# Output weights of the first group loaded in the last batch and split in place, a gate in four steps, and no conversion in a batch's first step

## The chip, the cores and the metric

The kernel runs on one core of a Trainium2 chip. The metric is device time in microseconds (us) of one execution, from the host's launch to the end, as the median of several runs. The engines are named as the profile names them: PE multiplies matrices, PEld loads its stationary operand, DVE, ACT and POOL are the vector, scalar and GpSimd engines, and SP issues most of the transfers. Each engine takes its instructions in the order in which they stand in its own queue.

## The reference

An attention, a mixture of experts over its output, and a last MLP. Cut to what matters here:

```python
def _attn_ref(q, k, v, p):                  # 4 batches, 8 heads, 576 tokens, head_dim 64
    p_packed = sm_attn(p, k, v)
    return sm_attn(q, p_packed, p_packed)

def _moe_ref(x, domain_probs, w1, w2):      # x (2304, 512), 4 experts, F = 1024
    p = domain_probs / (domain_probs.sum(-1, keepdims=True) + 1e-09)
    for e in range(E):
        h = np.maximum(x @ w1[e], 0.0)
        out += p[:, e:e + 1] * (h @ w2[e])

def _moe2_ref(x, w_in, w_out, s, b):        # w_in (512, 2048), w_out (2048, 512), both float64
    h = x @ w_in
    r = np.maximum(h, 0.0)
    g = s * (r * r) + b
    return (g @ w_out).astype(np.float32)
```

## The kernel before

Every float32 operand of a matmul is split into a high part (rounded to the multiplier's format by ACT) and a low part (the rest, by DVE or POOL), and each product is three matmuls: low by high, high by high, high by low.

**The expert loop** has 256 steps: 4 experts, 4 batches of 576 tokens, and 16 steps a batch (two halves of 288 tokens, 8 blocks of hidden columns each). A step runs the work woven into it (`run(i)`), then `m1` (L578), the first product of the step that comes two later, then `m2` (L605), the second product of its own step. `m1` ends with ACT's `hh` (L596) and DVE's `hl` (L597), which read the PSUM tile `h`. There are two such tiles, so the `m1` of two steps later cannot begin before that `hl` is done. A batch's last `m2` is followed by four evictions on DVE (`y`, L629). For an even batch the folded first weights (`fold_pair`, L419: PE, then ACT L434 and DVE L435 twice) are made during the batch before, one piece in each of eight steps, and the last piece falls in the batch's own first step.

**The conversion** (`last_weights`, L463) turns the float64 words of `w_in` and `w_out` into float32 by operations on integers. It has 32 tiles, each with a load and three parts: exponent (L485, L488), significand (L493 to L496), product (L502, POOL L505, and a store to `wi_dram` or `wo_dram`). The list `calm` holds the steps that may take a part. A part runs ahead of its step's `m1`, so DVE and ACT have it in their queues ahead of that step's `hh` and `hl`.

**The MLP** works in 4 groups of 512 hidden columns, each in 3 batches of 768 tokens. A batch has 14 products (`m3`, L715): 7 operands of a Strassen scheme, named 11, 12, s2, s3, s1, s4 and 22, for two column blocks `j`. I number the products through, p0 to p13 for the first batch, p14 to p27 for the second. p0 to p9 are run in the last steps of the expert loop (`EARLY`). DVE adds the products into `yy`. With s4 (p10, p11) and 22 (p12, p13) a piece of `yy` is complete and goes through the gate: ACT's Relu and Square (L703, L704), DVE's scale (L692), ACT's high part (L693), DVE's low part (L696). `go_on` (L708) takes every piece that is under way one step further after each product:

```python
    def gate(g, tp, j, c):
        nc.scalar.activation(y, y, AF.Relu)
        nc.scalar.activation(y, y, AF.Square)
        gg[g, tp, j, c] = t
        later.append([(gate_hi, y, t), (gate_lo, y, t)])
```

The output product `m4` (L757) of a batch is 72 matmuls: 6 tiles of 128 tokens, 12 matmuls each. They are dealt out from two products after the batch's end, some 5 behind each product: those of the first batch stand behind p16 to p29, those of the second behind p30 and on. The PSUM tiles `o` are two; in the first group ACT copies each to `o_sb` (L776), in the later groups DVE adds it there (L780). After the last product of all, PE runs what is left, 82 matmuls or so.

`m4` needs the group's output weights `wo`, four tiles. `load_wo` (L551) reads one from `wo_dram` on SP's queue into the raw tile `wor`, of which there are two, and `wo_parts` (L555) splits it: ACT L560 and POOL L561. For the first group both stand behind the end of the expert loop. SP's queue also holds the stores of the split operands `xs` to `xs_dram` (L684), each of which waits for DVE's low part (L683) of that operand.

Of the kernel before, what the change touches and what calls it, by code (L numbers as in the profile page):

```python
# [8 lines left out]
F32 = mybir.dt.float32  # L9
F32R = mybir.dt.float32r  # L10
U32 = mybir.dt.uint32
AF = mybir.ActivationFunctionType
ALU = mybir.AluOpType
# [6 lines left out]
def attention_experts_mlp_kernel(  # L20
# [25 lines left out]
    nc = tc.nc  # L46
    B, H, S, D = q.shape
    NP = p.shape[2]
    NT, DM = out.shape
    E, _, F = w1.shape  # L50
    DFF = w_out.shape[0]
    P = 128
    G = 2
    HT = S // 2
    NF = F // P
# [5 lines left out]
    T3 = 384  # L61
    NT3 = NT // T3
    NS = T3 // P
    FG = 4
# [4 lines left out]
    keep = ctx.enter_context(tc.tile_pool(name="keep", bufs=1))  # L69
# [10 lines left out]
    def f32(ap):  # L80
        return ap.bitcast(F32)
# [269 lines left out]
    w1_t, w1p, w2_t, wi_t, wo_t = {}, {}, {}, {}, {}  # L351
# [103 lines left out]
    NQ = FG // 2  # L455
# [5 lines left out]
    wo_dram = [dram.tile([P, DM], F32, name=f"wo_dram{fb}") for fb in range(DFF // P)]  # L461
# [46 lines left out]

        return load, exponent, significand, product

    tw, wop, wor = {}, {}, {}

    def load_wi(q):
        g = q // NQ
# [33 lines left out]
            nc.scalar.activation(t[:, j, 0], src, AF.Copy)  # L548
            nc.vector.tensor_tensor(out=t[:, j, 1], in0=src, in1=f32(t[:, j, 0]), op=ALU.subtract)

    def load_wo(fb):  # L551
        wor[fb] = gb.tile([P, DM], F32, tag="wor", bufs=2, name=f"wor{fb}")
        nc.sync.dma_start(out=wor[fb], in_=wo_dram[fb])

    def wo_parts(fb):  # L555
        pool, tag = (keep, "w1p") if fb // FG % 2 == 0 else (gb, "wo")
        t = pool.tile([P, 2, DM], F32R, tag=tag, bufs=FG, name=f"wo{fb}")
        hi, lo = wo_t[fb] = t[:, 0], t[:, 1]
        raw = wor.pop(fb)
        nc.scalar.activation(hi, raw, AF.Copy)  # L560
        nc.gpsimd.tensor_tensor(out=lo, in0=raw, in1=f32(hi), op=ALU.subtract)  # L561


    pb_t = {}
# [78 lines left out]
    xs, gg, o_acc, o_sb, sx, yy = {}, {}, {}, {}, {}, {}  # L643
# [44 lines left out]

    cur, later = {}, []

    def gate_hi(y, t):
        nc.vector.tensor_scalar(y, y, s_sb, b_sb, ALU.mult, ALU.add)  # L692
        nc.scalar.activation(t[:, 0], y, AF.Copy)  # L693

    def gate_lo(y, t):
        nc.vector.tensor_tensor(out=t[:, 1], in0=y, in1=f32(t[:, 0]), op=ALU.subtract)  # L696

    def gate(g, tp, j, c):


        y = yy[j][:, 2 * c : 2 * c + 2, :]
        t = gb.tile([P, 2, 2, T3], F32R, tag="gg", bufs=6, name=f"gg{g}{tp}{j}{c}")
        nc.scalar.activation(y, y, AF.Relu)  # L703
        nc.scalar.activation(y, y, AF.Square)  # L704
        gg[g, tp, j, c] = t
        later.append([(gate_hi, y, t), (gate_lo, y, t)])

    def go_on():  # L708
        for x in list(later):
# [5 lines left out]
    def m3(g, tp, k, j):  # L715
        op, name = OPS[k], f"{g}{tp}{k}{j}"
        n = cur["n"] = cur.get("n", -1) + 1
        if (g, tp) == (0, 0) and 2 * k + j < EARLY:
            ps = ps_m.tile([P, 512], F32, tag="m", name=f"h{name}")
        elif n % 3 == 0:  # L720
            ps = ps_h.tile([P, 512], F32, tag="h", name=f"h{name}")
        else:
            ps = ps_o.tile([P, 512], F32, tag="c", bufs=4, name=f"h{name}")
        ps = ps[:, :T3]
        w, x = wop[g, k][:, j], xs[g, tp, k]
        n = 0
        for m in range(HK):
            col = slice(m * P, (m + 1) * P)
            for a, z in ((1, 0), (0, 0), (0, 1)):
                nc.tensor.matmul(  # L730
                    ps, lhsT=w[:, a, col], rhs=x[:, z, m, :],
                    start=(n == 0), stop=(n == 3 * HK - 1),
                )
                n += 1
        if op == "11":
            yy[j] = wb.tile([P, 4, T3], F32, tag="yy", bufs=NQ, name=f"yy{name}")
            cur[j] = wb.tile([P, 2, T3], F32, tag="uv", bufs=NQ, name=f"uv{name}")
        y = yy[j]
        u, v = cur[j][:, 0], cur[j][:, 1]
        if op == "11":  # L740
            nc.scalar.activation(u, ps, AF.Copy)
        for dst, src in {
            "12": ((y[:, 0], u),),
            "s2": ((u, u),),
            "s3": ((v, u),),
            "s1": ((y[:, 1], u), (y[:, 3], v)),
            "s4": ((y[:, 1], y[:, 1]),),
            "22": ((y[:, 2], v),),
        }.get(op, ()):
            nc.vector.tensor_tensor(out=dst, in0=ps, in1=src, op=ALU.add)  # L750
        go_on()
        if op in ("s4", "22"):
            gate(g, tp, j, int(op == "22"))

    EARLY = 10
# [30 lines left out]
    with tc.manual_schedule():  # L786
# [3 lines left out]
        for gi in range(G):  # L790
# [4 lines left out]
            out=dp.rearrange("a j e -> a (j e)"),  # L795
            in_=probs.rearrange("(a j) e -> a (j e)", a=P),
# [88 lines left out]
        for gi in range(G):  # L885
# [3 lines left out]
        ua = [  # L889
            (e, bi, hf, f) for e in range(E) for bi in range(B) for hf in range(2) for f in range(NF)  # L890
        ]
# [15 lines left out]
        SB = 2 * NF  # L907

        def at(step, fn, *args):
            weave.setdefault(step, []).append((fn, args))  # L910
# [68 lines left out]
        for j in range(2):  # L979
# [1 line left out]

        calm = [
            e * B * SB + i for e in range(1, E) for i in range(3 * SB)
            if not SB + NF <= i < 2 * SB and (e < E - 1 or i < 2 * SB)
        ]
        tiles = [
            (w, g * FG + f) for g in range(NG) for w in ("wi", "wo") for f in range(FG)
# [15 lines left out]
        def pos(v):  # L1003

            return len(ua) + v - EARLY
# [1 line left out]
        for k in range(4, NK):  # L1007
            at(len(ua) - 8 + 2 * (k - 4), wop_parts, 0, k)
        for f in range(FG):
            at(pos(EARLY) + f, load_wo, f)  # L1010
            at(pos(EARLY) + 2 + f, wo_parts, f)
        for tp in range(NTP):
            u0 = tp * UP
            for d, what in enumerate(("s1", "s2", "s3")):
# [111 lines left out]
```

## Time and profile before

| what | value |
|---|---|
| runs, median (lowest to highest) | 1163.51 us (1163.32 to 1163.72) |
| the profiled execution's own time | 1165.72 us |
| its span, first to last instruction | 1163.9 us |
| busy: PE / DVE / ACT / POOL | 1114.5 / 697.9 / 453.9 / 278.5 us |
| mean granted PE clock, as a share of full speed | 0.988 |

PE is busy for 96% of the span, so what can still go are the stretches in which it waits, and those in which it runs at the lower clock. The profiled execution is 2.2 us longer than the median of the runs, and 1.8 us of its time lie outside its span.

### The profile page before, as it was taken

Reading aid. Unit: us, or ns where it says so; the run is one execution under the profiler, and the core shown is the slowest. Engines: PE = TensorE matmul, PEld = TensorE weight load, DVE = VectorE, ACT = ScalarE, POOL = GpSimd, SP = SyncE. Lnnn points to the kernel's source line nnn. Section 1 sums busy time; section 2 is a strip of 40 time slices with the busy share of each in tenths; the row PEclk is TensorE's granted clock in tenths of the full one; section 3 lists DMA queues with packets and bytes.
Section 4 is the critical chain, followed back from the end, with each engine's and each line's share of the span. In section 5 each row is a group of like instructions: output and inputs, shape, how many; then the busy total and the mean of one; then the engine's idle time right before and its main releaser. Section 6 shows DMA issues by size and latency. Waiting matters only on the chain.

```text
span 1163.9 us, 18380 instructions
## 1 busy us (share of the span) xinstructions
PE 1114.5 (96%) x7243; PEld 1043.4 (90%) x7243; DVE 697.9 (60%) x1276; ACT 453.9 (39%) x860; POOL 278.5 (24%) x337
## 2 busy tenths in 40 slices
PE   6899999999999999999999999979899999999997
PEld 4788998999999999999999999968789989998996
DVE  7767655466666576566576344557645666566554
ACT  3322222363343363343453333344454444334232
POOL 1421302133413342413244124425110200011000
PEclk9999999999999999999999999989899999999999
DMA  8622220223303324304233002235565655655532
GB/s 252 170 80 81 58 83 1 66 91 120 120 1 125 123 67 134 93 28 154 76 95 99 1 14 88 120 134 199 196 224 186 203 185 201 218 189 186 201 121 82
DMA packets 60150, 141.51 MB, mean 122 GB/s; under 512 B 8864, under 2 KB 29600, under 8 KB 60064
## 3 DMA queue, kind: packets, MB, share of 16 engines
q1 hardware_dynamic: 59792, 140.28, 36.9%
q8 instruction: 57, 0.93, 0.3%
q14 instruction: 29, 0.24, 0.1%
q10 hardware_dynamic: 272, 0.07, 0.0%
HBM read 110.66 MB, written 29.66 MB: 121 GB/s over the span
## 4 chain that ended last, share of the span: by engine, by line
PE 83%; DVE 7%; ACT 5%; issue 2%; DMA 1%; POOL 1%; SPq 0%; DVEq 0%; ACTq 0%; POOLq 0%
PE acc L614 33%; PE h L586 17%; PE o L764 14%; PE h L730 12%; PE pp L425 3%; ACT yy L703 1%; ACT yy L704 1%; PE s L288 1%; ACT gg L693 1%; PE pw L368 1%; DVE yy L692 1%; PE s L180 1%; DVE yy L750 1%; PE pv L234 1%; DMA w2r<-in_moe_w_dram 1%
## 5 line engine op out<-in xcount | busy, mean ns | idle before, releaser
L614 PE MATMUL acc<-hh,w2l 128*128 128x288 f32 x1024 | 304.3, 297 | 1.2 <-DVE sc L299 0.6
L614 PE MATMUL acc<-hl,w2h 128*128 128x288 f32 x1024 | 303.7, 297 | 0.0
L614 PE MATMUL acc<-hh,w2h 128*128 128x288 f32 x1024 | 303.5, 296 | 0.0
L586 PE MATMUL h<-a,w1p 128*128 128x288 f32 x1536 | 253.3, 301 | 10.4 <-DVE hl L597 7.7
L764 PE MATMUL o<-wo,gg 128*128 128x512 f32 x864 | 228.6, 397 | 21.2 <-POOL wo L561 9.8
L586 PEld LDWEIGHTS h<-a,w1p 128*128 128x128 f32 x1536 | 219.3, 190 | 19.8 <-DVE hl L597 9.1
L597 DVE SCALAR_TENSOR_TENSOR hl<-h,hh 128x288 fp32r<-128x288 f32 x256 | 116.5, 456 | 174.9 <-ACT hh L596 173.1
L764 PEld LDWEIGHTS o<-wo,gg 128*128 128x128 f32 x864 | 161.1, 189 | 50.3 <-POOL wo L561 11.9
L730 PE MATMUL h<-xs,wop 128*128 128x384 f32 x1008 | 206.0, 341 | 0.0
L614 PEld LDWEIGHTS acc<-hh,w2l 128*128 128x128 f32 x1024 | 193.3, 189 | 2.5 <-POOL w2l L450 1.2
L730 PEld LDWEIGHTS h<-xs,wop 128*128 128x128 f32 x1008 | 182.8, 190 | 13.1 <-DVE y L629 0.3
L614 PEld LDWEIGHTS acc<-hl,w2h 128*128 128x128 f32 x1024 | 193.8, 189 | 0.0
L614 PEld LDWEIGHTS acc<-hh,w2h 128*128 128x128 f32 x1024 | 193.6, 189 | 0.0
L596 ACT ACTIVATE hh<-h 128x288 fp32r<-128x288 f32 x256 | 103.9, 408 | 223.1 <-PE h L586 221.1
L640 POOL TENSOR_TENSOR x<-x,y 128x288 f32<-128x288 f32 (+2 forms) x144 | 87.7, 644 | 183.9 <-DVE y L629 183.9
L435 DVE TENSOR_TENSOR w1p<-pp,w1p 64x512 fp32r<-64x512 f32 x96 | 66.1, 688 | 53.7 <-ACT w1p L434 53.0
L703 ACT ACTIVATE yy<-yy 128x768 f32<-128x768 f32 x48 | 40.0, 834 | 115.3 <-DVE yy L750 115.3
L434 ACT ACTIVATE w1p<-pp 64x512 fp32r<-64x512 f32 x96 | 56.7, 591 | 70.2 <-DVE w1p L435 43.4
L750 DVE TENSOR_TENSOR yy<-h,uv 128x384 f32<-128x384 f32 x96 | 50.5, 551 | 26.7 <-PE h L730 26.3
L450 POOL TENSOR_TENSOR w2l<-w2r,w2h 128x512 fp32r<-128x512 f32 x32 | 41.6, 1300 | 86.8 <-ACT w2h L449 63.0
L696 DVE TENSOR_TENSOR gg<-yy,gg 128x768 fp32r<-128x768 f32 x48 | 51.2, 1066 | 18.2 <-ACT gg L693 18.2
L693 ACT ACTIVATE gg<-yy 128x768 fp32r<-128x768 f32 x48 | 40.6, 845 | 47.0 <-DVE yy L692 43.0
(361 smaller groups left out, 1100.9 us busy)
## 6 DMA issues: line engine op xcount, KB each, us to landing
xs<-xs_dram SPq DMA_DIRECT2D x63, 768.0 KB, 4.3
xs_dram<-xs SPq DMA_DIRECT2D x21, 768.0 KB, 3.3
w2r<-in_moe_w_dram SPq DMA_DIRECT2D x32, 256.0 KB, 2.8
w1r<-in_moe_w_dram SPq DMA_DIRECT2D x12, 512.0 KB, 4.0
pb<-pn_dram SPq DMA_DIRECT2D x16, 288.0 KB, 4.5
out_dram<-o_sb SPq DMA_DIRECT2D x17, 256.0 KB, 2.1
v<-in_v_dram SPq DMA_DIRECT2D x8, 512.0 KB, 5.7
wi<-wi_dram SPq DMA_DIRECT2D x8, 512.0 KB, 5.2
```

The costliest lines, as they stand in the source:

```text
L434: nc.scalar.activation(hi[r], t[r], AF.Copy)
L435: nc.vector.tensor_tensor(out=lo[r], in0=t[r], in1=f32(hi[r]), op=ALU.subtract)
L586: nc.tensor.matmul(t[:, :HT], lhsT=w[:, gi, col], rhs=a2[bi][:, x, gi, tok], start=(n == 0), stop=(n == 3 * G - 1),)
L596: nc.scalar.activation(xh, t[:, :HT], AF.Relu)
L597: nc.vector.scalar_tensor_tensor(out=xl, in0=t[:, :HT], scalar=0.0, in1=f32(xh), op0=ALU.max, op1=ALU.subtract)
L614: nc.tensor.matmul(acc[m][:, :HT], lhsT=w[:, col], rhs=x, start=(f == 0 and n == 0), stop=(f == NF - 1 and n == 2),)
L640: nc.gpsimd.tensor_tensor(out=dst, in0=dst, in1=y[:, a - t0 : z - t0], op=ALU.add)
L693: nc.scalar.activation(t[:, 0], y, AF.Copy)
L703: nc.scalar.activation(y, y, AF.Relu)
L730: nc.tensor.matmul(ps, lhsT=w[:, a, col], rhs=x[:, z, m, :], start=(n == 0), stop=(n == 3 * HK - 1),)
L750: nc.vector.tensor_tensor(out=dst, in0=ps, in1=src, op=ALU.add)
L764: nc.tensor.matmul(o_acc[i], lhsT=lhsT, rhs=w, start=(f == 0 and n == 0), stop=(f == FG - 1 and n == 2),)
```

## The change

Three things are changed.

The list `calm` leaves out each batch's first step (`i % SB`). All 32 tiles still fit, and the conversion now ends at step 215 instead of 207.

The first group's `wo` tiles are loaded in steps 250 and 253 of the expert loop, by transfers that ACT's queue issues, and split from step 254 on. In all groups the raw weights land in the low half of their own tile; ACT writes the high half from it, and POOL subtracts in place. The raw tiles `wor` are gone.

The gate has four steps instead of Relu and Square at once and two more: Relu with Square one product later, scale after two, high part after three, low part after four. Since a piece is then still under way when the next batch begins, `yy` and `uv` are allocated once and not anew for each batch.

```diff
-    def load_wo(fb):
-        wor[fb] = gb.tile([P, DM], F32, tag="wor", bufs=2, name=f"wor{fb}")
-        nc.sync.dma_start(out=wor[fb], in_=wo_dram[fb])
-
-    def wo_parts(fb):
+    def load_wo(fb, eng=nc.sync):
         pool, tag = (keep, "w1p") if fb // FG % 2 == 0 else (gb, "wo")
         t = pool.tile([P, 2, DM], F32R, tag=tag, bufs=FG, name=f"wo{fb}")
-        hi, lo = wo_t[fb] = t[:, 0], t[:, 1]
-        raw = wor.pop(fb)
-        nc.scalar.activation(hi, raw, AF.Copy)
-        nc.gpsimd.tensor_tensor(out=lo, in0=raw, in1=f32(hi), op=ALU.subtract)
+        eng.dma_start(out=f32(t[:, 1]), in_=wo_dram[fb])
+        wo_t[fb] = t[:, 0], t[:, 1]
+
+    def wo_parts(fb):
+        hi, lo = wo_t[fb]
+        nc.scalar.activation(hi, f32(lo), AF.Copy)
+        nc.gpsimd.tensor_tensor(out=lo, in0=f32(lo), in1=f32(hi), op=ALU.subtract)
...
-    def gate_hi(y, t):
-        nc.vector.tensor_scalar(y, y, s_sb, b_sb, ALU.mult, ALU.add)
-        nc.scalar.activation(t[:, 0], y, AF.Copy)
...
+    def gate_act(y, key):
         nc.scalar.activation(y, y, AF.Relu)
         nc.scalar.activation(y, y, AF.Square)
-        gg[g, tp, j, c] = t
-        later.append([(gate_hi, y, t), (gate_lo, y, t)])
+
+    def gate_scale(y, key):
+        nc.vector.tensor_scalar(y, y, s_sb, b_sb, ALU.mult, ALU.add)
+
+    def gate_hi(y, key):
+        name = "gg" + "".join(map(str, key))
+        t = gg[key] = gb.tile([P, 2, 2, T3], F32R, tag="gg", bufs=6, name=name)
+        nc.scalar.activation(t[:, 0], y, AF.Copy)
+
+    def gate_lo(y, key):
+        t = gg[key]
+        nc.vector.tensor_tensor(out=t[:, 1], in0=y, in1=f32(t[:, 0]), op=ALU.subtract)
+
+    def gate(g, tp, j, c):
...
+        later.append([(fn, y, (g, tp, j, c)) for fn in (gate_act, gate_scale, gate_hi, gate_lo)])
...
-        if op == "11":
-            yy[j] = wb.tile([P, 4, T3], F32, tag="yy", bufs=NQ, name=f"yy{name}")
-            cur[j] = wb.tile([P, 2, T3], F32, tag="uv", bufs=NQ, name=f"uv{name}")
+        if j not in yy:
+            yy[j] = wb.tile([P, 4, T3], F32, name=f"yy{j}")
+            cur[j] = wb.tile([P, 2, T3], F32, name=f"uv{j}")
...
-            if not SB + NF <= i < 2 * SB and (e < E - 1 or i < 2 * SB)
+            if i % SB and not SB + NF <= i < 2 * SB and (e < E - 1 or i < 2 * SB)
...
         for f in range(FG):
-            at(pos(EARLY) + f, load_wo, f)
-            at(pos(EARLY) + 2 + f, wo_parts, f)
+            at(len(ua) - (6 if f == 0 else 3), load_wo, f, nc.scalar)
+            at(len(ua) - (2 if f == 0 else -f), wo_parts, f)
```

In the changed kernel Relu, Square, scale, high and low part stand on L691, L692, L695, L700 and L704, the two halves of the split on L559 and L560, the load on L554.

The first place is DVE's queue around the first step of the third expert's first batch, before (the four `y` are the evictions, `w1p` the last folded weights, `wo5a` and `wo5e` the conversion):

```order
L629 TENSOR_TENSOR y_4951<-acc_4637,pb_4147 128x288
L435 TENSOR_TENSOR w1p_4910<-pp_2031_4954,w1p_4910 64x512
L435 TENSOR_TENSOR w1p_4909<-pp_2031_4954,w1p_4909 64x512
L493 TENSOR_SCALAR wo5a<-wo5raw 128x512
L495 TENSOR_SCALAR wo5e<-wo5e 128x512
L496 SCALAR_TENSOR_TENSOR wo5e<-wo5raw,wo5e 128x512
L597 SCALAR_TENSOR_TENSOR hl_4982<-h_4974,hh_4981 128x288
```

The same place with the change:

```order
L628 TENSOR_TENSOR y_4938<-acc_4624,pb_4134 128x288
L435 TENSOR_TENSOR w1p_4897<-pp_2031_4941,w1p_4897 64x512
L435 TENSOR_TENSOR w1p_4896<-pp_2031_4941,w1p_4896 64x512
L596 SCALAR_TENSOR_TENSOR hl_4964<-h_4956,hh_4963 128x288
L493 TENSOR_SCALAR wo4a<-wo4raw 128x512
L495 TENSOR_SCALAR wo4e<-wo4e 128x512
```

The `hl` for which a later `m1` waits now stands directly behind the folded weights, and the conversion behind it, in the next step.

The second place is ACT's queue from the last `hh` of the expert loop to the gates of p10 and p11, before (`yy_8650` and `yy_8700` are the two column blocks):

```order
L596 ACTIVATE hh_8898<-h_8891 128x288
L682 ACTIVATE xs_8947<-x_2_1450 128x768
L703 ACTIVATE yy_8650<-yy_8650 128x768
L704 ACTIVATE yy_8650<-yy_8650 128x768
L682 ACTIVATE xs_9008<-x_2_1450 128x768
L693 ACTIVATE gg_9003<-yy_8650 128x768
L703 ACTIVATE yy_8700<-yy_8700 128x768
L704 ACTIVATE yy_8700<-yy_8700 128x768
L560 ACTIVATE wo_9025<-wor_8993 128x512
L693 ACTIVATE gg_9022<-yy_8700 128x768
```

With the change, and from the three later loads on:

```order
L554 DMA wo_8895<-wo_dram_99 128x512
L595 ACTIVATE hh_8906<-h_8899 128x288
L559 ACTIVATE wo_8783<-wo_8783 128x512
L681 ACTIVATE xs_8957<-x_2_1450 128x768
L559 ACTIVATE wo_8891<-wo_8891 128x512
L681 ACTIVATE xs_9013<-x_2_1450 128x768
L691 ACTIVATE yy_8650<-yy_8650 128x768
L692 ACTIVATE yy_8650<-yy_8650 128x768
L559 ACTIVATE wo_8893<-wo_8893 128x512
L691 ACTIVATE yy_8700<-yy_8700 128x768
L692 ACTIVATE yy_8700<-yy_8700 128x768
```

The first two splits now stand ahead of the first gate, and the high part of p10's piece behind the Square of p11's, the fourth split and one more `xs`.

The third place is ACT's queue in the first group's second batch, between the gates of p24 to p27, before (`o_sb` is the copy of a finished output tile, here the fourth and the fifth of the batch ahead):

```order
L703 ACTIVATE yy_9098<-yy_9098 128x768
L704 ACTIVATE yy_9098<-yy_9098 128x768
L776 ACTIVATE o_sb_9278<-o_9237 128x512
L693 ACTIVATE gg_9273<-yy_9098 128x768
L703 ACTIVATE yy_9077<-yy_9077 128x768
L704 ACTIVATE yy_9077<-yy_9077 128x768
L682 ACTIVATE xs_9309<-s_2_9200 128x768
L693 ACTIVATE gg_9301<-yy_9077 128x768
L703 ACTIVATE yy_9098<-yy_9098 128x768
L704 ACTIVATE yy_9098<-yy_9098 128x768
L776 ACTIVATE o_sb_9278<-o_9280 128x512
```

With the change:

```order
L691 ACTIVATE yy_8650<-yy_8650 128x768
L692 ACTIVATE yy_8650<-yy_8650 128x768
L780 ACTIVATE o_sb_9264<-o_9229 128x512
L691 ACTIVATE yy_8700<-yy_8700 128x768
L692 ACTIVATE yy_8700<-yy_8700 128x768
L681 ACTIVATE xs_9292<-s_2_9192 128x768
L700 ACTIVATE gg_9304<-yy_8650 128x768
L691 ACTIVATE yy_8650<-yy_8650 128x768
L692 ACTIVATE yy_8650<-yy_8650 128x768
L780 ACTIVATE o_sb_9264<-o_9266 128x512
```

The fourth copy stood behind two Relu-Square pairs and one high part, and now stands behind one pair; the fifth stood behind all four pairs and three high parts, and now stands behind three pairs and one high part.

## Rows read from the trace of the kernel before

**Rows 1.** Waits of PE over the span: total us, times, longest.

```profile
PE o L764 <- POOL wo L561: 9.8, 4, 3.7
PE o L764 <- ACT o_sb L776: 7.8, 3, 4.6
PE h L586 <- DVE hl L597: 7.7, 6, 2.2
PE o L764 <- DVE o_sb L780: 3.5, 4, 2.1
```

**Rows 2.** Timeline, expert 2's first batch: start us, us, instruction [idle before <-releaser].

```profile
427.71 0.69 DVE L435 TENSOR_TENSOR w1p<-pp,w1p 64x512 fp32r<-64x512 f32 x1 [0.66 <-ACT w1p L434]
...
428.42 1.57 DVE L493 TENSOR_SCALAR wo5a<-wo5raw 128x512 uint32<-128x512 uint32 x1
...
431.73 1.38 PE L586 MATMUL h<-a,w1p 128*128 128x288 f32 x6 [2.16 <-DVE hl L597]
```

**Rows 3.** Stretches: us, busy us of PE, PEld, DVE, ACT, POOL, then clock, DMA.

```profile
432.00:436.00 4.00, 4.00 (x20) 4.00 (x20) 2.86 (x6) 1.07 (x3) 1.28 (x1) 0.57 0.20 70
676.00:690.00 14.00, 14.00 (x107) 13.89 (x106) 6.81 (x14) 4.42 (x10) 8.63 (x7) 1.00 0.07 23
776.00:784.00 8.00, 4.68 (x12) 3.25 (x12) 4.13 (x5) 4.55 (x8) 1.60 (x2) 0.57 0.48 164
824.00:828.00 4.00, 4.00 (x12) 3.53 (x11) 2.80 (x4) 3.98 (x9) 0.85 (x1) 0.50 0.26 105
```

**Rows 4.** Timeline of PE, products p9 to p18 and the first output products.

```profile
763.80 8.88 PE L730 MATMUL h<-xs,wop 128*128 128x384 f32 x48
776.38 1.11 PE L764 MATMUL o<-wo,gg 128*128 128x512 f32 x3 [3.70 <-POOL wo L561]
...
788.91 2.02 PE L730 MATMUL h<-xs,wop 128*128 128x384 f32 x6
```

**Rows 5.** Timeline of ACT in the same stretch.

```profile
767.48 0.84 ACT L703 ACTIVATE yy<-yy 128x768 f32<-128x768 f32 x1 [6.86 <-DVE yy L750]
...
769.11 0.83 ACT L682 ACTIVATE xs<-x 128x768 fp32r<-128x768 f32 x1
772.02 0.84 ACT L693 ACTIVATE gg<-yy 128x768 fp32r<-128x768 f32 x1 [2.08 <-DVE yy L692]
...
774.38 0.61 ACT L560 ACTIVATE wo<-wor 128x512 fp32r<-128x512 f32 x1
...
785.18 0.47 ACT L741 ACTIVATE uv<-h 128x384 f32<-128x384 f32 x1
```

**Rows 6.** Timeline of DVE in the same stretch.

```profile
766.90 0.55 DVE L750 TENSOR_TENSOR yy<-h,yy 128x384 f32<-128x384 f32 x1
771.32 0.67 DVE L692 TENSOR_SCALAR yy<-yy,s_sb,b_sb 128x768 f32<-128x768 f32 x1
...
772.90 0.96 DVE L696 TENSOR_TENSOR gg<-yy,gg 128x768 fp32r<-128x768 f32 x1 [0.44 <-ACT gg L693]
```

**Rows 7.** SP's queue: two issues of the raw weights, and its longest wait, 700 to 860.

```profile
776.36 3.52 SPq L553 DMA_DIRECT2D wor<-wo_dram  x2
...
SPq L684 <- DVE xs L683: 96.8, 17, 19.2
```

**Rows 8.** Timeline of all engines around the second batch's gates, p24 to p31.

```profile
804.45 0.56 DVE L750 TENSOR_TENSOR yy<-h,yy 128x384 f32<-128x384 f32 x1
...
817.08 1.87 POOL L667 TENSOR_TENSOR s<-x,s 128x768 f32<-128x768 f32 x1 [3.71 <-DVE xs L683]
817.38 2.37 DVE L696 TENSOR_TENSOR gg<-yy,gg 128x768 fp32r<-128x768 f32 x1
...
823.37 2.50 PE L764 MATMUL o<-wo,gg 128*128 128x512 f32 x5 [4.62 <-ACT o_sb L776]
```

**Rows 9.** Timeline of the last batch's end: PE and DVE.

```profile
1136.00 1.23 PE L730 MATMUL h<-xs,wop 128*128 128x384 f32 x6
...
1146.30 13.90 PE L764 MATMUL o<-wo,gg 128*128 128x512 f32 x60 [2.11 <-DVE o_sb L780]
```

More of the change, by code (lines that the diff above doesn't have):

```diff
@@ L509, in last_weights @@
         return load, exponent, significand, product
-    tw, wop, wor = {}, {}, {}
+    tw, wop = {}, {}
     def load_wi(q):
@@ L689, in attention_experts_mlp_kernel @@
     cur, later = {}, []
-    def gate_hi(y, t):
+    def gate_act(y, key):
+        nc.scalar.activation(y, y, AF.Relu)
+        nc.scalar.activation(y, y, AF.Square)
+    def gate_scale(y, key):
         nc.vector.tensor_scalar(y, y, s_sb, b_sb, ALU.mult, ALU.add)
+    def gate_hi(y, key):
+        name = "gg" + "".join(map(str, key))
+        t = gg[key] = gb.tile([P, 2, 2, T3], F32R, tag="gg", bufs=6, name=name)
         nc.scalar.activation(t[:, 0], y, AF.Copy)
-    def gate_lo(y, t):
+    def gate_lo(y, key):
+        t = gg[key]
         nc.vector.tensor_tensor(out=t[:, 1], in0=y, in1=f32(t[:, 0]), op=ALU.subtract)
@@ L701, in gate @@
         y = yy[j][:, 2 * c : 2 * c + 2, :]
-        t = gb.tile([P, 2, 2, T3], F32R, tag="gg", bufs=6, name=f"gg{g}{tp}{j}{c}")
-        nc.scalar.activation(y, y, AF.Relu)
-        nc.scalar.activation(y, y, AF.Square)
-        gg[g, tp, j, c] = t
-        later.append([(gate_hi, y, t), (gate_lo, y, t)])
+        later.append([(fn, y, (g, tp, j, c)) for fn in (gate_act, gate_scale, gate_hi, gate_lo)])
     def go_on():
```

## The prediction

> **What bounds the kernel now.** The page says first that PE is busy for 96% of the span, and the followed chain that the end hangs on PE. A change elsewhere can therefore only win where PE stands still or runs at the lower clock, and the first view to read is that of PE's waits [rows 1]. Four kinds of wait bear on the change: 9.8 us in 4 waits for POOL's half of the `wo` split, 7.8 in 3 for ACT's copy to `o_sb`, 7.7 in 6 for DVE's `hl`, and 3.5 in 4 for DVE's add to `o_sb`: 28.8 us together.
>
> The timeline then shows what each wait is made of. For `hl` I read a batch's first step [rows 2]. DVE ends the last folded weights at 428.40 and goes straight on to the conversion's first operation, 1.57 us, which stood ahead of `hl` in its queue; PE waits 2.16 us and begins at 431.73. The third reading is the granted clock in stretches around each wait [rows 3]. After this wait the clock is 0.57 for 4 us, so it costs another 4.00 x 0.43 = 1.7 us. It is 0.57 again in 776 to 784, and 0.50 in 824 to 828, each time behind a long wait of PE; 1.2 GHz is the lower of the two levels, and both readings lie at it or are a mixture with it.
>
> For `wo` I read PE, ACT and DVE between p9 and p18 [rows 4 to 6] and SP's queue [rows 7]. The last two raw tiles are issued at 776.36 only, the two before them are not split before the gate of p10, and PE stands 3.70 us before 776.38 and three times more up to the end of p18 at 788.91 + 2.02 = 790.93. For `o_sb` I read the gates of p24 to p27 [rows 8]: PE asks for an output tile at 823.37 - 4.62 = 818.75 and gets it at 823.37. The last is the end [rows 9]: the last product is done at 1137.23, and PE waits 2.11 us before the last 60 output matmuls.
>
> **The change, part by part.** The work itself hardly changes: as many Relu, Square, scale, high and low parts, splits and conversions as before, at the same sizes. What changes is when they stand in a queue, so each part is worth what its wait and its clock were worth.
>
> *No conversion in a first step.* The fold's last piece remains, and `hl` follows it. In the stretch 676 to 690, which covers the first step of the last expert's third batch, a fold without a conversion, PE is busy 14.00 of 14.00 us at clock 1.00 [rows 3]. I take the whole 7.7 us [rows 1] and the 1.7 of clock: **9.4**. The conversion ends eight steps later, in steps of kinds that carry such parts now. Their cover is PE's work of a step; without it one conversion operation costs up to the 1.57 us of [rows 2].
>
> *The weights of the first group.* The load leaves SP's queue, whose entries wait in order for DVE (96.8 us in 17 waits, [rows 7]), and goes to ACT's. The trace shows no such issue on ACT. Below I bound it at nothing, above by SP's row, 3.52 us for two [rows 7], so 1.8 each; ACT is idle for 61% of the span, and in the expert loop it is ahead of PE, so I take nothing. Behind the four issues stand only `hh` of later steps; the upper bound with nothing to hide it would be 7 us, but each `m1` has a step of PE's work between it and its `hh`'s reader. The Trainium skill speaks against a gain here: in "DMA: Bandwidth & Descriptors", section "Issuing engines are not separate DMA queues", it says that issuing from several engines saves the issuing sequencer's time and opens no other path to memory. By that the raw tiles would come no faster once issued; the row on SP is about when they are issued.
>
> Now the first batch's boundary, laid on the queues by hand from row durations. On ACT a Relu with Square takes 769.11 - 767.48 = 1.63, `xs` 0.83, a high part 0.84, a split 0.61, `uv` 0.47 [rows 5]; on DVE an add 0.55, scale 0.67, low part 0.96 [rows 6]. p10's piece is whole at 766.90 + 0.55, as before. ACT then runs: p10's pair to 769.11, third split 769.72, p11's pair 771.35, fourth split 771.96, `xs` 772.79, p10's high part 773.63, p12's pair 775.26, `uv` 775.73, p11's high part 776.57, p13's pair 778.20, `xs` 779.03. DVE runs p10's low part to 775.93 and, behind the low part of that `xs`, p11's to 780.95. PE's first two output matmuls need high parts alone and can start at 773.63 instead of 776.38; three more follow 775.93, then p17, three more up to about 778.4, a wait to 780.95 for p11's low part, and p18 to 782.5 at the full clock, 784.1 if the stretch is again at about half. Against 790.93 this is 8.4 or 6.8; I take **7.3**, near the second, because waits of about 2.5 us remain and the waits of that size in [rows 2, 3] had a lower clock behind them. The splits on POOL end well ahead, the first two standing before the gate.
>
> In this layout DVE's low part is late if POOL's addition for `s4` (1.87 us) meets it. In [rows 8] a low part beside such an addition takes 2.37 us instead of the 0.96 of [rows 6], and ends with it or after it. The Trainium skill, "SBUF — State Buffer", section "SBUF: two separate sides", states that DVE and GpSimd share a port pair under a lock that blocks the other for the whole instruction; the trace agrees. By that rule p10's low part would end near 776.6, and the sum would be 0.7 smaller.
>
> *The gate in four steps.* Its worth lies in the copies that stand behind gate pieces on ACT. In the second batch p24's add is done at 805.0 [rows 8]. A product with its five output matmuls takes 8.88/8 + 5 x 13.90/60 = 2.27 us [rows 4, 9]. A tile has 12 matmuls, dealt out from p16 on, so the fourth tile is done one product behind p24, at about 807.2. ACT copies it to 807.8 (0.6, an estimate from the 0.61 of an equally wide split), then p25's pair 809.4, `xs` 810.2, p24's high part 811.1, p26's pair 812.7, and the fifth tile's copy is done at 813.3. PE asks at 818.75, so this wait is gone with 5 us to spare. The last low parts are then the next that can be late: p25's ends about 819.7, when PE comes to it. I take all three waits for the copy, 7.8 [rows 1], and the clock of 0.50 in 824 to 828, 2.0 [rows 3]: **9.8**.
>
> At the end of the program the fifth tile's add stands behind the last low part in DVE's queue, and with four steps ahead of it; I place it at about 1144.5 against the present start of PE at 1146.30 [rows 9]: **1.8**. Of the rest of the 3.5 in [rows 1], 1.4 us at three earlier boundaries, I take half, **0.6**: DVE's order there is changed less.
>
> The new price of the gate is that a low part ends two products later, and two of a batch's four pieces are not ready when it ends. The m4 that needs them stands 2 products behind it, and is dealt out over 14; by the layout p11's low part is due one product, 2.27 us, or more before PE reaches it at the later boundaries, where no split is in the queue. I take nothing for it, and its upper bound is a rival. Persistent `yy` and `uv` would make DVE's first write of a batch wait for the gate's scale of the batch before; p0 to p9 stand between, and a `yy` tile had two buffers in all before, so I take nothing.
>
> The sum is 9.4 + 7.3 + 9.8 + 1.8 + 0.6 = 28.9 us. The profiled execution would go from 1165.72 to 1136.8, and the median, 2.2 lower, from 1163.51 to **1134.6**.
>
> **The rivals.** *A: the gate's chain is bound by ACT's and DVE's rate, not by order.* Each batch brings four pieces within five products, and ACT is full in 824 to 828 (3.98 of 4.00, [rows 3]). Then the fifth copy stays late, the low parts behind it too, and 9.8 is not won: 1144.4. Against it: the layout has 5 us to spare.
>
> *B: fold and evictions alone make the first step late.* DVE has 4 evictions and two `w1p` of 0.69 [rows 2] there with or without the conversion. Then the 9.4 is not won: 1144.0. The stretch 676 to 690 is against it.
>
> *C, slower: the gate's low part becomes late at every boundary.* There are 12. From 28.9/12 = 2.4 us each, it decides the sign; one wait of 3 us at 11 of them would give 1134.6 + 33 = 1167.6. For it: after the last product nothing is left to cover two more steps. Against it: about a product to spare, above.
>
> *D: the load on ACT's queue brings the weights no earlier,* by the rule on issuing engines: the four transfers share with the `xs` loads what they share now. Then boundary one stays, 7.3 is not won, and the time is 1141.9. Against it: SP holds the last two issues back to 776.36 [rows 7], and the change has no such wait.
>
> **How the numbers follow.** Forecast 0.70, A 0.13, B 0.05, D 0.05, C 0.05 at its full price and 0.02 at one that cancels the gain. The best that the bounds allow is 0.8 more at the later boundaries, 1.1 at the first without the lower clock, and about 1 elsewhere (the tail without a wait): 1131.7, rounded down to 1131. Above, the range takes in A, B and D, with the 0.7 of the lock and 1 us of the issues on A: 1146. What is left out is C with 0.07 and some 0.1 of mishaps that add up. The forecast's own range is 1131 to 1138. A change of 0.2%, 2.3 us, is about the least that can be told from none: faster 0.93, same 0.02, slower 0.05.
>
> **What the profile of after would show.** No wait for `hl` above 0.5 us and a full clock after each first step; else B. PE's first output matmul 2.75 us earlier against the product before it, at about 764 if the expert loop is 9.4 shorter, and no wait for POOL's split; else D. No wait for ACT's `o_sb` in the first group; else A. In place of these, a wait of some 2.5 us for DVE's `gg` at the first boundary, and none of that kind at the others; if these are there with 2 us or more, C. The last 60 matmuls begin within 0.4 us of those before them. I am wrong if PE's total of waits falls by less than 15 us, or if the clock falls at places that have none now.

## The result and the profile after

The changed kernel takes 1131.0 us (median of 4 runs, 1130.81 to 1131.1), the kernel before 1163.62 beside it (1163.32 to 1165.4). The ratio is 0.9716, with a 95% interval from 0.97 to 0.9733: faster, by 32.6 us between the medians. (The ratio is that of the means; the medians alone give 0.9720.) The forecast was 28.9 less and 1134.6, with a range from 1131 to 1146. More was won than that: the median is 3.6 us below the forecast, and 0.9716 of the 1163.51 from which the forecast started is 1130.5, just under the range. The profiled execution takes 1130.81 us, with a span of 1129.0.

The page of after, first the share of PE and its clock:

```profile
span 1129.0 us, 18395 instructions
PE 1106.7 (98%) x7243; PEld 1040.2 (92%) x7243; DVE 691.8 (61%) x1276; ACT 453.9 (40%) x860; POOL 284.8 (25%) x337
PEclk9999999999999999999999999998999999999999
```

PE's waits over the span (total us, times, longest), to be read beside [rows 1]:

```profile
PE o L768 <- DVE gg L704: 3.1, 1, 3.1
...
PE o L768 <- DVE o_sb L784: 0.9, 1, 0.9
PE o L768 <- ACT gg L700: 0.8, 1, 0.8
...
PE h L585 <- DVE hl L596: 0.2, 1, 0.2
```

Of the 28.8 us of four kinds, the waits for POOL's split and for ACT's copy are gone altogether, those for `hl` are down to 0.2 (in the kernel's first steps, not at a batch's first step), those for DVE's add to 0.9. In their place stand 3.1 for p10's low part and 0.8 for its high part, both at the first boundary. So 28.8 us of waits became 5.0.

Where the time came from is read by laying the starts of the same products in PE's timeline beside each other. The table gives them in us from the span's start, and the gain in each stretch, which is the length of that stretch before less its length after.

| stretch | before, from and to | after, from and to | gain | forecast |
|---|---|---|---|---|
| attention, up to the eighth `m2` | 0 to 70.23 | 0 to 68.65 | 1.58 | 0 |
| expert loop, up to p0 | 70.23 to 734.50 | 68.65 to 721.91 | 11.01 | 9.4 |
| first boundary, p0 to p21 | 734.50 to 796.32 | 721.91 to 776.46 | 7.27 | 7.3 |
| copies, p21 to p52 | 796.32 to 876.95 | 776.46 to 845.97 | 11.12 | 9.8 |
| later groups, p52 to the end of p167 | 876.95 to 1137.23 | 845.97 to 1104.09 | 2.16 | 0.6 |
| the end, behind p167 | 1137.23 to 1160.20 | 1104.09 to 1125.27 | 1.79 | 1.8 |

The 1.58 in front of the change is not of it (below). Without it the stretches sum to 33.3 us. The two profiled executions differ by 34.9, the medians by 32.6, since the one of before was 2.1 longer than its median.

At the first boundary the timeline of PE after reads, beside [rows 4]:

```profile
760.88 0.70 PE L768 MATMUL o<-wo,gg 128*128 128x512 f32 x2 [0.79 <-ACT gg L700]
764.67 1.65 PE L768 MATMUL o<-wo,gg 128*128 128x512 f32 x3 [3.09 <-DVE gg L704]
766.12 2.12 PE L734 MATMUL h<-xs,wop 128*128 128x384 f32 x6
768.03 1.97 PE L768 MATMUL o<-wo,gg 128*128 128x512 f32 x5
769.84 1.20 PE L734 MATMUL h<-xs,wop 128*128 128x384 f32 x6
```

and the stretches (us, busy us of PE, PEld, DVE, ACT, POOL, clock, DMA), beside [rows 3]:

```profile
424.00:428.00 4.00, 4.00 (x33) 4.00 (x32) 3.94 (x7) 1.32 (x3) 1.42 (x2) 1.00 0.01 4
762.00:766.00 4.00, 1.33 (x3) 1.14 (x4) 3.21 (x3) 2.91 (x5) 1.33 (x1) 0.58 0.49 197
766.00:770.00 4.00, 4.00 (x13) 3.52 (x13) 3.00 (x3) 2.08 (x4) 1.90 (x1) 0.57 0.31 129
796.00:804.00 8.00, 8.00 (x42) 7.19 (x41) 6.70 (x11) 6.46 (x13) 1.92 (x3) 1.00 0.25 100
```

The product that waited 2.16 us in the third expert's first batch now falls into the stretch 424 to 428; that stretch and the second boundary (796 to 804) have a busy PE at the full clock. Only the first boundary still has a wait and a lower clock behind it; p17's six matmuls take 2.12 us there, p18's 1.20.

### The profile page after: what moved, and what is told of

It reads as the page before. It is cut to its first block, busy times and chain, and to the rows that moved or that the text cites. A ratio compares the mean times of both kernels' runs of the same rounds, so it can differ in the third digit from the quotient of the medians.

```text
span 1129.0 us, 18395 instructions
## 1 busy us (share of the span) xinstructions
PE 1106.7 (98%) x7243; PEld 1040.2 (92%) x7243; DVE 691.8 (61%) x1276; ACT 453.9 (40%) x860; POOL 284.8 (25%) x337
## 4 chain that ended last, share of the span: by engine, by line
PE 93%; DVE 3%; DMA 1%; ACT 1%; issue 1%; POOL 1%; SPq 0%; DVEq 0%; ACTq 0%
PE acc L613 36%; PE h L585 18%; PE o L768 17%; PE h L734 15%; PE pp L425 3%; PE s L288 1%; PE pw L368 1%; PE s L180 1%; PE pv L234 1%; DVE kT L150 1%; DMA k<-in_k_dram 1%; DMA v<-in_v_dram 0%; DVE qT L150 0%; POOL w2l L450 0%; DVE yy L695 0%
## 5 line engine op out<-in xcount | busy, mean ns | idle before, releaser
L768 PE MATMUL o<-wo,gg 128*128 128x512 f32 x864 | 224.9, 394 | 4.8 <-DVE gg L704 3.1
L691 ACT ACTIVATE yy<-yy 128x768 f32<-128x768 f32 x48 | 40.3, 839 | 109.8 <-DVE yy L754 109.8
L704 DVE TENSOR_TENSOR gg<-yy,gg 128x768 fp32r<-128x768 f32 x48 | 49.5, 1032 | 2.7 <-ACT gg L700 2.5
L560 POOL TENSOR_TENSOR wo<-wo 128x512 fp32r<-128x512 f32 x16 | 24.3, 1522 | 103.3 <-ACT wo L559 103.3
```

Source lines behind the costliest of these rows:

```text
L768: nc.tensor.matmul(o_acc[i], lhsT=lhsT, rhs=w, start=(f == 0 and n == 0), stop=(f == FG - 1 and n == 2),)
```

## Experiments

**Each part alone.** Three kernels take one of the three edits each, and a fourth is the kernel before once more. The edits are pieces of the diff above. `k_only`, no conversion in a first step:

```diff
-            if not SB + NF <= i < 2 * SB and (e < E - 1 or i < 2 * SB)
+            if i % SB and not SB + NF <= i < 2 * SB and (e < E - 1 or i < 2 * SB)
```

> The kernel before with the list of steps alone changed (no conversion in a batch's first step). Theory 1 (each part is worth its own stretches, and a wait costs about 0.2 us more than its idle row because the first matmul behind it runs longer): 10.8 us less, 1152.8. Theory 2 (the prediction's term, idle rows and clock alone): 9.4 less, 1154.2. If the folded weights alone make the step late: no change, 1163.6.

`w_only`, the early weights:

```diff
-            at(pos(EARLY) + f, load_wo, f)
-            at(pos(EARLY) + 2 + f, wo_parts, f)
+            at(len(ua) - (6 if f == 0 else 3), load_wo, f, nc.scalar)
+            at(len(ua) - (2 if f == 0 else -f), wo_parts, f)
```

(with `load_wo` and `wo_parts` as changed).

> The kernel before with the first group's output weights loaded and split early, gate and conversion as before. Theory 1 (parts add up): the first boundary gains what it gained in the whole change, 8.7, so 1154.9. Theory 3 (at the first boundary weights and gate work only together, because ACT's chain of gate pieces comes late behind the splits): under 4 us less, above 1159.6.

`g_only`, the gate:

```diff
-        later.append([(gate_hi, y, t), (gate_lo, y, t)])
+        later.append([(fn, y, (g, tp, j, c)) for fn in (gate_act, gate_scale, gate_hi, gate_lo)])
```

(with its four functions, and `yy` and `uv` allocated once).

> The kernel before with the gate in four steps alone. Theory 1: the second and third boundary 10.8, the later groups 2 and the end 1.5 less, 14.3 in all, so 1149.3, and the first boundary still waits about 9.8 us for POOL's split. Theory 3 (weights and gate interact at the first boundary): more or less than this by over 2 us, with the difference lying in the first boundary.

`again`, no edit:

> The kernel before once more, for a second profile. Theory 1: the 2.4 us wait for the first folded weights and the 1.4 for ACT's tile in the attention are of that one execution, and this one has a span of about 1161.8 with waits of 0.5 and 0.2 there. Rival: they come back at the same size, and the change removed them.

| kernel | median us | ratio to before, interval | loop | first boundary | copies | later | end |
|---|---|---|---|---|---|---|---|
| before | 1163.37 | | | | | | |
| `k_only` | 1153.07 | 0.9915, 0.99 to 0.993 | 10.74 | 0.08 | 0.08 | 0.05 | 0.0 |
| `w_only` | 1161.4 | 0.9984, 0.9972 to 0.9997 | 0.03 | 2.41 | -2.38 | 0.04 | 0.0 |
| `g_only` | 1145.38 | 0.9849, 0.9832 to 0.9866 | -0.12 | 3.88 | 11.12 | 2.16 | 1.74 |
| `again` | 1164.75, one run | | 1.25 | -0.77 | -1.70 | 0.06 | 0.0 |

The last five columns are gains by stretch against the profiled execution of before, worked out as in the table of the result. What stands in the line of `again`, up to 1.7 us, is what two executions of the same kernel differ by.

The loop goes to one part alone, and the copies, the later groups and the end to the gate. `k_only` gains 10.3 us between the medians, 8.1 to 11.6 by the interval, so its time alone doesn't tell Theory 1 (10.8) from Theory 2 (9.4); the single waits do, below. The loop of `again` is 1.25 us shorter without an edit, because one wait of 1.21 us, at 601.26 in the execution before, did not come in it.

At the first boundary weights and gate add to 6.29 where the change gains 7.27. That they help each other by the 1 us between is not shown, since `again` is 0.77 off there with no edit. The weights alone bring 2.4 there and not the 7.27 of the change (the 8.7 of the expectation), and by the medians 2.0 in all, 0.3 to 3.3 by the interval; in this Theory 3 was right. The profiled execution of `w_only` is the slowest of its ten, 1165.62. The gate alone gains 18.0 between the medians, 3.7 more than Theory 1 had, and the difference lies in the first boundary, as Theory 3 had it for that run; but that both work only together is wrong, since the gate brings 3.9 at this boundary with the late weights. Why is read in PE's timeline of `w_only`:

```profile
773.93 0.70 PE L763 MATMUL o<-wo,gg 128*128 128x512 f32 x2 [1.05 <-ACT gg L692]
...
784.03 1.22 PE L763 MATMUL o<-wo,gg 128*128 128x512 f32 x2 [5.96 <-DVE gg L695]
```

and in that of DVE:

```profile
779.88 1.39 DVE L682 TENSOR_TENSOR xs<-s,xs 128x768 fp32r<-128x768 f32 x1 [3.77 <-ACT xs L681]
781.20 0.54 DVE L749 TENSOR_TENSOR yy<-h,uv 128x384 f32<-128x384 f32 x1
781.67 2.31 DVE L695 TENSOR_TENSOR gg<-yy,gg 128x768 fp32r<-128x768 f32 x1
```

With the weights in time, a low part of the old gate takes the place of the split as the last thing to come: DVE waits 3.77 us for ACT's `xs`, which stands behind two pairs, two splits and a high part, and the low part is next in DVE's queue. In `g_only` it is the other way round: its high parts no longer wait on ACT for DVE's scale with the later splits behind them, so the splits come early enough with the late loads too, and no wait for POOL is left there (the last split starts on POOL at 777.74, the wait for the low part ends at 782.36).

Of the loss of 2.38 at the copies in `w_only`, 0.5 is a longer wait for the first copy (1.18 instead of 0.67). The loss of 1.70 in `again` has no edit behind it. The waits for the copy are 7.8 us in all in `again`, as in [rows 1]; what differs is the clock. In `again`, at the third boundary:

```profile
856.00:860.00 4.00, 2.20 (x5) 1.82 (x6) 1.91 (x3) 3.97 (x8) 1.28 (x1) 0.65 0.07 28
860.00:864.00 4.00, 4.00 (x20) 3.65 (x20) 1.65 (x4) 0.77 (x2) 1.29 (x1) 0.92 0.61 167
```

In the profiled execution of before both stretches are at 1.00, and in `w_only` at 0.77 and 0.81. So the same wait may or may not have a lower clock around and behind it, which is part of why executions of one kernel differ: 1160.51 to 1167.37 over all runs of before in this study. As to the attention, `again` came to the eighth `m2` at 68.08, `k_only` at 68.37, `behind` at 67.37, before at 70.23, after at 68.65, and the changed kernel in a later execution at 70.48: that stretch scatters by 3 us with no edit in it. Of the two waits that the expectation of `again` names, the one for the folded weights is 0.9 there, and the one for ACT's tile came back at 1.4, so its Theory 1 held in part. Neither is a gain of the change: `k_only`, which leaves the attention as it was, has neither, and `after_sp`, with the whole change, has 0.8 and 1.4.

**Order or amount in a first step.** `behind` leaves every conversion part in its step, and issues those of a first step behind that step's `m1`:

```diff
+                if i % SB or d < 0:
+                    at(i, fn)
+                else:
+                    tail.setdefault(i, []).append(fn)
...
             advance()
+            for fn in tail.pop(i, ()):
+                fn()
             m2(*u)
```

> The kernel before, in which a conversion part of a batch's first step stands behind that step's first product instead of ahead of it; no part is moved to another step. Theory 1 (only the order ahead of the low part in DVE's and ACT's queues matters): the same as leaving the first step out, 1153.1. Theory 4 (the first step has too much work for DVE, whatever its order): the wait comes back one product later, and at most half of the 10.3 us is won, above 1158.

It takes 1157.22 us, ratio 0.9947 (0.9927 to 0.9966): 6.5 us less than before between the medians, 4.0 to 8.5 by the interval, where `k_only` has 10.3. Its profiled execution is the fastest of the four, 1155.08, and there the loop gains 8.42 of the 10.74 of `k_only`. So most of it is the order: the long waits are gone with the same work in the step. The rest is the load of DVE; a wait comes back one product later, as Theory 4 had it, but with 0.3 us at most. Neither theory's time was met. The short waits show what a wait costs. PE's waits of `behind`, of which three lie in the expert loop:

```profile
PE h L586 <- DVE hl L597: 1.0, 4, 0.3
```

and one of them in PE's timeline:

```profile
589.88 0.97 PE L586 MATMUL h<-a,w1p 128*128 128x288 f32 x6
...
592.73 1.05 PE L586 MATMUL h<-a,w1p 128*128 128x288 f32 x6 [0.28 <-DVE hl L597]
...
595.25 0.95 PE L586 MATMUL h<-a,w1p 128*128 128x288 f32 x6
```

Two steps take 595.25 - 589.88 = 5.37 us. The same two in `k_only`, with no wait:

```profile
589.22 0.95 PE L586 MATMUL h<-a,w1p 128*128 128x288 f32 x6
...
593.99 0.96 PE L586 MATMUL h<-a,w1p 128*128 128x288 f32 x6
```

take 4.77. A wait of 0.28 cost 0.60. Counted from the starts of the second products, the three waits of 0.25, 0.31 and 0.28 cost 0.51, 0.58 and 0.55, and one of 0.11, too short for the row, cost 0.38. The row counts idle time from the end of the last matmul as the profile gives it, and the profile models these ends. In its rows matmuls run into each other: those of the second product start 0.13 us apart and last 0.29 each, so behind a wait 0.16 of overlap is missing, and the group of six takes 1.05 instead of 0.95. The two make 0.26, an estimate from these rows. The larger waits of before give nearly the same. The timeline of before, at a first step with no lower clock behind it:

```profile
258.29 0.96 PE L586 MATMUL h<-a,w1p 128*128 128x288 f32 x6
262.81 1.06 PE L586 MATMUL h<-a,w1p 128*128 128x288 f32 x6 [1.98 <-DVE hl L597]
265.29 0.95 PE L586 MATMUL h<-a,w1p 128*128 128x288 f32 x6
```

and the first and the last of the same three products after:

```profile
256.58 0.95 PE L585 MATMUL h<-a,w1p 128*128 128x288 f32 x6
...
261.33 0.95 PE L585 MATMUL h<-a,w1p 128*128 128x288 f32 x6
```

7.00 us became 4.75, so the wait of 1.98 was worth 2.25. That of 1.10 at 346.59 is worth 1.33, and that of 0.67 for the first copy 0.93, read from the same products before and after. **Each wait costs its row and about 0.27 us.**

**The queue of the loads.** `after_sp` is the changed kernel with the four loads back on SP's queue, in the new steps:

```diff
-            at(len(ua) - (6 if f == 0 else 3), load_wo, f, nc.scalar)
+            at(len(ua) - (6 if f == 0 else 3), load_wo, f)
```

> The changed kernel with the four early loads on SP's queue in place of ACT's, in the same steps. Prediction (SP's queue holds them back behind stores that wait for DVE): the splits come late, and the first boundary loses some of its 7.3 us, 1133 to 1138. Theory 5 (the step in which they are issued matters, not the queue): 1131.0.

1130.7 us (0.9717, 0.9698 to 0.9736), and 7.61 at the first boundary: the queue makes no difference that the runs can show, as Theory 5 has it. SP does hold three of the four loads back; in its queue, behind two stores of which the second waits for DVE:

```profile
736.34 7.19 SPq L683 DMA_DIRECT2D xs_dram<-xs  x2
743.62 1.84 SPq L554 DMA_DIRECT2D wo<-wo_dram  x3
```

ACT's issue of the same three begins at 741.12 in the changed kernel, where p0 starts at 721.91; here p0 starts at 722.67, so SP is 1.7 us later. The first of the three lands at 748.01, and the split that stands next on ACT starts at 748.70, at the same distance from p0 as in the changed kernel: the loads were early enough, by 0.7 us. ACT's queue brought the issue 1.7 us forward and won no time. This agrees with the Trainium skill, "DMA: Bandwidth & Descriptors", section "Issuing engines are not separate DMA queues": another issuing engine saves the sequencer's time alone.

**What is left at the first boundary.** Three kernels move one thing each. `split_early` has the three later splits ahead of all gates:

```diff
-            at(len(ua) - (2 if f == 0 else -f), wo_parts, f)
+            at(len(ua) - (2 if f == 0 else 2 - f), wo_parts, f)
```

> The changed kernel with the second to fourth split one to two steps earlier, ahead of all gates. Theory 6 (what is left at the first boundary, waits of 0.8 and 3.1 us and a clock of 0.57 behind them, is the chain of ACT's queue, in which two splits of 0.61 stand): p10's high part 1.2 us earlier, its low part at least as much, and the long wait under 2 us; 1.2 to 5 us less than the changed kernel, 1126 to 1129.8. Rival (POOL's addition and splits hold DVE back by its port, wherever the splits stand): within 1 us of 1131.0.

`gate_three` calls the scale in the step of Relu and Square:

```diff
-        later.append([(fn, y, (g, tp, j, c)) for fn in (gate_act, gate_scale, gate_hi, gate_lo)])
+        later.append([(fn, y, (g, tp, j, c)) for fn in (gate_act, gate_hi, gate_lo)])
```

> The changed kernel with the scale in the same step as Relu and Square, so three steps. Theory 7 (the fourth step is what makes p10's low part late at the first boundary, and the copies need only the deferred high part): first boundary up to 4 us better, the rest as in the changed kernel, 1127 to 1131. Rival (DVE then waits at the head of its queue for ACT's Square, and ACT's copies stand behind high parts again): a wait for the copy or for the low part at later boundaries, 1132 or more.

`xs_later` splits the second batch's operands one product later:

```diff
-                at(pos(u0 + 2 * k) - 5 - (tp == 0), xs_parts, tp, k)
+                at(pos(u0 + 2 * k) - 5 - (tp == 0) + (tp == 1), xs_parts, tp, k)
```

> The changed kernel with the split of the first group's second batch's operands one product later, so that p11's scale stands ahead of one of them in DVE's queue and POOL's addition, which waits for that split, starts after the scale. Theory 8 (the 3.1 us wait at the first boundary is DVE's 1.9 us scale beside POOL's addition, and the split that it stands behind): p10's low part 2 to 3 us earlier, the wait under 1.2 us and no lower clock behind it, first boundary 2 to 4 us better, 1127 to 1129. Rival (ACT's chain sets it): the same wait, 1131.

| kernel | median us | ratio, interval | first boundary | end |
|---|---|---|---|---|
| changed kernel (table of the result) | 1131.0 | 0.9716, 0.97 to 0.9733 | 7.27 | 1.79 |
| `split_early` | 1130.21 | 0.9715, 0.9695 to 0.9734 | 8.17 | 1.75 |
| `gate_three` | 1134.46 | 0.975, 0.9729 to 0.9771 | 7.21 | -1.56 |
| `xs_later` | 1131.64 | 0.9723, 0.9706 to 0.9741 | 7.04 | 1.79 |

None of them takes the wait away. DVE in the changed kernel:

```profile
760.03 1.41 DVE L682 TENSOR_TENSOR xs<-s,xs 128x768 fp32r<-128x768 f32 x1 [2.37 <-ACT xs L681]
761.36 0.54 DVE L754 TENSOR_TENSOR yy<-h,uv 128x384 f32<-128x384 f32 x1
761.83 1.92 DVE L695 TENSOR_SCALAR yy<-yy,s_sb,b_sb 128x768 f32<-128x768 f32 x1
763.67 0.94 DVE L704 TENSOR_TENSOR gg<-yy,gg 128x768 fp32r<-128x768 f32 x1
```

and POOL beside it:

```profile
761.52 1.81 POOL L666 TENSOR_TENSOR s<-x,s 128x768 f32<-128x768 f32 x1 [0.89 <-DVE xs L682]
```

p10's low part starts at 763.67, though its high part on ACT was done at 760.74. Ahead of it DVE waits 2.37 us for ACT's `xs`, and p11's scale takes 1.92 beside POOL's addition where it takes 0.67 alone. In `split_early` the wait falls to 2.7 us, a second of 1.5 comes up behind it, and one of 0.55 for an eviction `y` ahead of both. These are 4.7 us of waits, more than the 3.9 of the changed kernel, but the clock is 1.00 throughout: 0.9 better in the trace, and not to be told from the changed kernel by the medians (`after_sp`, with the splits of the changed kernel, has 7.61). The high part ends at 760.87, no earlier than in the changed kernel, since p10's gate begins at 755.98 instead of 754.89, behind the evictions. In `xs_later` the scale does come first (760.05), but then DVE waits 1.71 us at the operand's split with the low part behind it, and PE waits 3.4. In `gate_three` PE waits 5.0 us for the same low part: DVE first waits 2.06 us for ACT's Square, then 0.57 for ACT's `xs`, and the low part itself takes 2.32 us beside POOL's addition; and at the end the old waits for DVE's add are back, 0.30 and 2.13, which is its loss of 3.35. So the 0.9 of `split_early` is the clock's, whether by the order or by chance, and not that of Theory 6, whose earlier high part did not come; Theories 7 and 8 won nothing; the times that the three rivals named are those that were measured. As I read these rows, the low part is late by two causes in a row, ACT's `xs` and POOL's addition, and an order that gets p11's scale out of the way leaves the low part itself to one of them. No kernel that removes both was run.

**The end.** `tail_mix` deals the last matmuls of the batch ahead out between the last gate steps:

```diff
         while later:
             go_on()
+            second(8)
         todo += behind(ub[-1])
```

> The changed kernel with the last output matmuls of the batch ahead dealt out between the last gate steps, so that DVE's add of its last tile stands ahead of the last two low parts. Theory 9 (a wait costs its idle row and 0.27 more, since the matmul behind it does not overlap the one ahead): the 0.9 us wait goes, and the end comes 1.2 us earlier, 1129.8. Rival (the row alone): 0.9; or a wait for a low part takes its place: 1131.

It takes 1128.68 us (0.9695, 0.9677 to 0.9712), and the changed kernel in the same series 1131.92 (0.9723, 0.9703 to 0.9744); the intervals overlap. In its trace the end gains 2.98 instead of 1.79, 1.19, near the 1.17 that a wait of 0.90 and 0.27 make, as Theory 9 has it; of the rest between the two profiled executions, 1129.04 and 1132.84, 2.2 lie in front of the change, up to the eighth `m2`, in the stretch that scatters. What the second run of the changed kernel was to show:

> The changed kernel once more, beside the three others on one chip: 1131.0, and its waits of 3.1, 0.9 and 0.8 us as before.

Its waits are 3.1, 0.9 and 0.8 again. `best` has `split_early`, `xs_later` and `tail_mix` together:

> The changed kernel with the earlier splits, the later operand split and the dealt out end together. If they add up: 1131.0 less 0.9, 3 and 1.2, so 1126; if the first two remove the same wait: 1127.

1129.48 us (0.9704, 0.9687 to 0.972): the end is that of `tail_mix`, 2.98, the first boundary 7.49 with a wait of 3.4, so neither of its two sums, 1126 and 1127, came true: the first two edits won nothing here. `tail_mix` alone has the lowest median of this study, though its interval overlaps with that of `best`.

## Why the prediction was right in kind and short in size

The places, the cause at most of them and the order of the sizes held. The sum was 4.4 us short of the 33.3 in the traces, and 3.7 of the 32.6 between the medians, and the time fell out of the range at its lower end. The step that failed is the price of a wait, "each part is worth what its wait and its clock were worth", by which a wait was worth its idle row. The runs showed about 0.27 us more for each: in the traces 1.6 of the shortfall in the loop, 1.1 at the copies and 1.1 in the later groups. The "best that the bounds allow", 1131.7, had no room for it.

- *No conversion in a first step*, 9.4 forecast, 11.01 measured (10.74 alone, 10.3 between medians). The mechanism was right: `behind` shows that the order decides. The term that was too small is "I take the whole 7.7 us and the 1.7 of clock", with each wait at its idle row. Six waits at 0.27 more make 1.6, and 9.4 + 1.6 = 11.0. Rival B is out.
- *The copies*, 9.8 forecast, 11.12 measured. The layout was right: no wait for ACT's copy is left, and the fifth copy is done at 793.11, 4.7 us before PE comes for the tile at 797.81. Three waits at 0.27 make 0.8. Another 0.3 is a fourth wait, of 0.04 us and so not in [rows 1]: p41 to p42 takes 849.12 to 851.63 before and 821.24 to 823.45 after. The last 0.2 is the clock: the long wait with what follows it, p30 to p32, takes 817.53 to 829.04 before and 796.77 to 801.16 after, 7.1 us, which is 4.62 and 0.27 for the wait and 2.2 for the clock, where 2.0 was taken. Rival A is out.
- *The later boundaries*, 0.6 forecast, 2.16 measured. The 1.4 was misread: its waits are 0.52 at 954.68, 0.60 at 1049.71 and 0.30 at 1141.19, and the third lies behind the last product, in the end. Taking half was wrong too, since both waits went, and with 0.27 each they make 1.7. The other 0.5 lies in two waits below what the rows list, at 959.79 and 1054.82, worth 0.29 and 0.27.
- *The first boundary*, 7.3 forecast, 7.27 measured, but not by the path laid out; the agreement is luck. The layout had PE's first output matmul 2.75 us earlier against the product before it; it came 2.9 earlier (776.38 - 760.88 = 15.50, less 12.59 of the loop and the attention). It had p10's low part end 1.3 us earlier than it did, because it gave p11's scale 0.67 us; the scale took 1.92 beside POOL's addition. The forecast had priced the meeting of the two at 0.7, on a low part. The Trainium skill, "SBUF — State Buffer", section "SBUF: two separate sides", states that of these two engines the one that starts first holds the port pair they share, where both need it, for its whole instruction; the trace agrees in the main, the scale starts 0.3 us behind POOL's addition and ends 0.4 us after it. On the other side, the second wait of 2.5 us did not come, since PE was at a clock of 0.57 and so reached it later; `split_early`, at 1.00, has one of 1.5 there. And the prediction put the gain under the weights, which alone bring 2.4 of it, the gate alone 3.9.
- *ACT's queue for the loads* was taken as the cause of the earlier weights, against rival D. The sign named for D, a wait for POOL's split, says little: `g_only` has the late loads and no such wait. The weights came early, but by the step: `after_sp` has them on SP with the same time. The reason given was wrong. The bound of 1.8 us for an issue was misread as well: the 3.52 of [rows 7] spans two issues of 0.32 each and SP's wait between them, and on ACT an issue took 0.33 to 0.45.
- *The end*, 1.8 forecast, 1.79 measured; the forecast that the last 60 matmuls follow within 0.4 us was wrong, they waited 0.90, because DVE's add still stood behind two low parts. That wins 1.21 of the 2.11; the old wait of 0.30 ahead of it went as well, with its 0.27. So the right sum is luck here too.
- *C, the slower rival*, had its wait at one boundary of twelve only, and there 3.1 us. At the others the trace has no wait for a low part.

## What to carry over

When the waits of a full engine are added up to price an edit, count them as well as sum them: here each cost 0.27 us above its idle row, and with a dozen waits this was the largest part of the error in the traces. Waits too short for the table count as well. A wait that an edit removes should be followed by asking what stands next in the same queue: the weights alone gained 2.4 us of 7.3, since a low part was late right behind them. And where the gain is put down to a queue or to a step, the two can be tested apart by one word in the code.

## What the runs showed of the hardware that was not expected

The lower clock behind a wait is not sure to come. The third boundary's 2.5 us wait had 1.00 behind it in one execution of the kernel before and 0.65 and 0.92 in another; a wait of 0.8 and 3.1 us in the changed kernel had 0.58 and 0.57 around and behind it, while 2.7 and 1.5 in `split_early` had 1.00. What a kernel's scatter comes from besides stays open: `gate_three`, with few waits, ran from 1131.8 to 1135.65 in four runs, the changed kernel from 1130.0 to 1134.24 in eight. So a gain under 2 us was read here from traces, stretch by stretch, and not from medians.
